# Layer 2 of a two-layer MLP after attention: visits over a rolling window of weight pairs, and additions shared out between VectorE and GpSimd by waiting time

## The chip, the cores and the metric

The kernel runs on one core of a Trainium2 chip. The metric is the device time of one execution in microseconds (us). Names: PE is TensorE (PEld its weight loads), ACT ScalarE, DVE VectorE, POOL GpSimd, SP the queue that issues the transfers.

## What is computed

Attention over 2304 tokens (4 batches of 576, 8 heads of 64) gives x [2304, 512]. Then two layers follow, in float32:

```
x = _moe_ref(x, w_in, w_out, alpha)     # h = x @ w_in; g = max(h,0) + alpha*min(h,0); g @ w_out
y = _moe2_ref(x, w_in, w_out)           # h = x @ w_in; g = h if h>0 else exp(h)-1;    g @ w_out
```

Both layers go from 512 to 2048 features and back to 512. The weights arrive as 64-bit floats.

## The kernel before

**Numbers in two halves.** A float32 product is made of three TensorE products: every operand x is split into a high part xh (a copy by ACT, rounded by its type) and a low part xl = x - xh (a subtraction on another engine). So each tile that PE reads costs one ACT copy and one subtraction of 128x512.

**Layer 1** takes tokens in groups of 288; each of its steps s is one block of 128 features. Its element-wise work on DVE is r (the leaky ReLU) and gl (the low part of g), two instructions a step.

**Layer 2** works on *pairs* of feature blocks (256 features) and on groups of 512 tokens; the last group has 256. There are 8 pairs (NP2 in the change) and 5 groups (`NB2`; the small one is `HALF`). The up-projection of one pair and one group is a *unit* u: seven products by Strassen's scheme in Winograd's form (`upf`, L1610 on), then the exponential and the split of g (`th_el2`, `th_el3`), and the down-projection (`down2`) with accumulation over the pairs of a turn in four PSUM banks. A unit of the small group is done plainly (`uph`, `th_elh`). On DVE a full unit begins with the sum m (m<-s,bank), then e and three c, three n and two gl. PE may go on to the unit's last three products only when m, e and c are there. Units are numbered from u0; four units (`NJ`) make a *turn*, and there are ten turns, so 40 units.

**Two passes.** `turns` is a list of (h, z): pass h uses pairs 0 to 3 (h=0) or 4 to 7 (h=1), z is the token group. In pass 0 every group's partial output is stored to DRAM (`osp`), in pass 1 it is read back and added (`th_os`, `th_fin2`). The last group of pass 0 is the first of pass 1, and its prepared input is kept (`xof`), so nine inputs are prepared.

**Weight pairs.** SBUF holds four pairs (`wslot`). A pair's preparation (`th_conv_in`, `th_conv_out`) is: four transfers of raw 64-bit weights, 512 KB each (`th_ldw2`); for each of the four an ACT op and two DVE ops that turn 64 bits into 32 (`decode`: cp, then cw); four sums S of 128x256 for Strassen's scheme; and six splits (four wi, two wo). In pass 0 the four slots stay in use until the fifth turn has passed over them, so pairs 4 to 7 are all loaded and prepared while that turn and the next run (units u16 to u22).

**Token groups.** `th_x2` loads a group's input, makes four differences xt and seven splits xq; eleven subtractions of 128x512.

**Who subtracts.** The sums S, the wi splits, the xt, the xq and the eight additions x of group 0's partial input are on POOL, the wo splits and all of the element-wise chain on DVE.

**What sets the order.** The program is put in order when it is built: threads (`spawn`, with a priority) are advanced by a table of engine times in `_Clock`, and each engine then executes its list strictly in that order, waiting on semaphores. Threads of layer 2's chain have priorities near -100; the weights and groups have 2 and more, and fill what is free. The lines of the profile are all L246 because one helper (`_Engine`) issues everything; operations are told apart by their tiles.

Of the kernel before, what the change touches and what calls it, by code (L numbers as in the profile page):

```python
# [36 lines left out]
XR = 11  # L37
WARM = True
# [19 lines left out]
class _Clock:  # L58
# [10 lines left out]
    def __init__(self):  # L69
        self.cols, self.gear = {}, []  # L70
        self.t = dict.fromkeys(("PE", "ACT", "DVE", "SP", "DMA", "POOL"), 0.0)
        self.t["SP"] = 560.0
        self.hw = 0.0
        self.seen = {}
# [84 lines left out]
    def op(self, eng, cost, share, outs, ins, wait=0.0):  # L159
        outs, ins = [self.span(a) for a in outs], [self.span(a) for a in ins]  # L160
        t = max(self.t[eng], self.deps(eng, outs, ins) + wait)
        if share is not None:
            cost += 42.0 if share > 0.9 and self.share < 0.9 else 0.0
            self.share = share
        end = t + cost if share is None else self.pe(t, cost, share)
        self.note(eng, outs, ins, end)
        self.t[eng] = self.cur["t"] = end
        self.cur["on"] = eng
# [32 lines left out]
class _Engine:  # L201
# [3 lines left out]
    def cost(self, op, kw, args):  # L205
        if op == "transpose":
            return int(args[1].shape[0]) / 1.2 + 3, int(args[1].shape[0]) * int(args[0].shape[0]) / 16384
        if op == "matmul":
            n, m = _free(kw["out"]), int(kw["out"].shape[0])
            share = int(kw["lhsT"].shape[0]) * m / 16384  # L210
            if kw["lhsT"].dtype == BF16:
                return n / 2.4, share
            if kw["lhsT"].dtype == F32R:
                return max(n * 0.4375 + 7, m / 1.2 + 3), share
            if int(kw["lhsT"].shape[0]) == D and int(kw["lhsT"].offset) >= D * int(kw["lhsT"].ap[0][0]):
                return 8.0, share
# [12 lines left out]
        if op == "reciprocal":
            return 68 + n * 6.25, None  # L230
        fast = sb and op in ("tensor_scalar", "tensor_copy")
        ptr = op == "scalar_tensor_tensor" and not isinstance(kw["scalar"], (int, float))
        return 68 + n * (0.52 if fast else 1.0417) + (60 if ptr else 0), None

    def __getattr__(self, op):
        fn = getattr(self.eng, op)

        def call(*args, **kw):
            if op == "dma_start":
                self.clock.dma(kw["out"], kw["in_"])  # L240
            else:
                outs = [kw[k] for k in ("out", "accum_out") if k in kw] + list(args[:1])
                ins = [a for k, a in kw.items() if k not in ("out", "accum_out") and hasattr(a, "ap")]
                wait = 0.6 * int(kw["lhsT"].shape[1]) if op == "matmul" else 0.0
                self.clock.op(self.name, *self.cost(op, kw, args), outs, ins + list(args[1:]), wait)
            return fn(*args, **kw)  # L246
# [4 lines left out]
def fused_kernel(ctx: ExitStack, tc: tile.TileContext, qk, vt, vl, ql, kl, vb, w_in1, w_out1, alpha,  # L251
# [72 lines left out]
    def load_w(key, slot=None):  # L324
        ly, nm, f = key
# [422 lines left out]
    order = [z for z in range(1, HALF - 1)] + [0, HALF, HALF - 1]  # L748
    turns = [(0, z) for z in order] + [(1, z) for z in [HALF - 1] + list(range(HALF - 1)) + [HALF]]
# [44 lines left out]
    def advance(th):  # L794
# [19 lines left out]
        if w:  # L814
            if w[0] == "bank":
                return False
            t = ck.t[w[0]]
# [416 lines left out]
    def part(t, x, eng):  # L1234
        n = _free(x)
        ACT.activation(out=t[:, 0, 0:n], in_=x, func=AF.Copy)
        yield (eng.name,)
        eng.tensor_tensor(out=t[:, 1, 0:n], in0=x, in1=t[:, 0, 0:n].bitcast(F32), op=ALU.subtract)

    def th_conv_in(h, j):  # L1240
        f = h * NF // 2 + 2 * j
        for z in range(2):
            yield from decode((2, "i", f + z))
        x, y = tmp.pop((2, "i", f)), tmp.pop((2, "i", f + 1))
# [3 lines left out]
        for o, p, q, op in ((0, a21, a22, ALU.add), (1, S[:, 0], a11, ALU.subtract), (2, a11, a21, ALU.subtract),  # L1248
                            (3, a12, S[:, 1], ALU.subtract)):
            yield ("POOL",)  # L1250
            POOL.tensor_tensor(out=S[:, o], in0=p, in1=q, op=op)
        st["W", h, j] = w = []
        for z, src in enumerate((x, S[:, 0:2].rearrange("p s c -> p (s c)"), S[:, 2:4].rearrange("p s c -> p (s c)"), y)):
            yield "key", "fr", h, wslot[j][z]
            yield ("ACT",)
            w.append(w_slot(wslot[j][z], f"wi{h}{j}{z}"))
            yield from part(w[z], src, POOL)
# [3 lines left out]
        finish("wi", h, j)  # L1261

    def th_conv_out(h, f):
        key = (2, "o", h * NF // 2 + f)
        yield from decode(key)
        yield ("ACT",)
        st["Wo", h, f] = w_slot(wslot[f // 2][4 + f % 2], f"wo{h}{f}")
        yield from part(st["Wo", h, f], tmp.pop(key), DVE)
        put("cw")
        finish("wo", h, f)  # L1270

    def th_ldw2():
        for h in range(2):
            for j in range(NJ):
                for nm, z in (("i", 0), ("i", 1), ("o", 0), ("o", 1)):
                    slot = wslot[j][z + (4 if nm == "o" else 0)]
                    yield "key", "fr", h, slot
                    yield ("DMA",)
                    key = (2, nm, h * NF // 2 + 2 * j + z)
                    load_w(key, slot)  # L1280
                    finish("ld", key)
                    ck.cur["t"] = now[0]
# [114 lines left out]
    def th_x2(i, z):  # L1397
# [20 lines left out]
        if not z:  # L1418
            for kt in range(KT):
# [3 lines left out]
                yield ("POOL",)  # L1423
                POOL.tensor_tensor(out=t[:, kt, :G1], in0=t[:, kt, :G1], in1=p[:, :G1], op=ALU.add)
# [3 lines left out]
        def diff(x, y, out=None):  # L1428
            o = cp["pool"].tile([128, 2, U2], F32, tag="xt", name="xt", bufs=2) if out is None else out
            POOL.tensor_tensor(out=o, in0=x, in1=y, op=ALU.subtract)  # L1430
            return o

        def split2(k, x):
# [15 lines left out]
            yield ("POOL",)  # L1449
            POOL.tensor_tensor(out=q[:, 1], in0=x, in1=q[:, 0].bitcast(F32), op=ALU.subtract)  # L1450
# [7 lines left out]
        yield ("POOL",)  # L1458
        t1 = diff(b12, b11)
        yield ("POOL",)  # L1460
        t2 = diff(b22, t1)
# [3 lines left out]
        yield ("POOL",)  # L1465
        t3 = diff(b22, b12)
# [3 lines left out]
        yield ("POOL",)  # L1470
        diff(b21, t2, t2)
# [90 lines left out]
    def uph(u, f):  # L1562
        i, j = divmod(u, NJ)
        h, z = turns[i]
        bk = bank[(5, 6)[u % 2] if f else (4, 7)[u % 2]][:, :U2]
        xi = xof[i]
        if not f:
# [3 lines left out]
            run_until("wi", h, j)  # L1571
# [3 lines left out]
        at(done["wi", h, j], done["x2", xi, 0], done["x2", xi, 1])  # L1575
        for k in range(2):
            q = st["x2", xi, k]
            for a in range(2):
                for b, (pw, px) in enumerate(P3):
                    PE.matmul(out=bk,  # L1580
                              lhsT=st["W", h, j][3 * f][:, HL[pw], (2 * k + a) * 128:(2 * k + a + 1) * 128],
# [9 lines left out]
    def up2(u, late):  # L1591
        i, j = divmod(u, NJ)
        h, z = turns[i]
# [4 lines left out]
        if late and i == NB2 - 1:  # L1598
            for z in range(4):
                ck.cur["t"] = ck.t["PE"]  # L1600
                finish("fr", 1, wslot[j][z])

    def upf(u, late):
        i, j = divmod(u, NJ)
        h, z = turns[i]
# [3 lines left out]
        if not late:  # L1609
# [3 lines left out]
            run_until("wi", h, j)  # L1613
        xi = xof[i]
        for k, (w, o) in enumerate(PROD):
# [6 lines left out]
            t = [done["wi", h, j], done["x2", xi, k]]  # L1622
# [4 lines left out]
            for a in range(2):  # L1627
                for b, (pw, px) in enumerate(P3):
                    PE.matmul(out=outs[k], lhsT=st["W", h, j][w][:, HL[pw], o + a * 128:o + (a + 1) * 128],
# [3 lines left out]
            if j == NJ - 1 and not (i + 1 < len(turns) and xof[i + 1] == xi):  # L1633
# [6 lines left out]
    def down2(u, f):  # L1640
        i, j = divmod(u, NJ)
        h, z = turns[i]
        run_until("gu", u, f)
        run_until("wo", h, 2 * j + f)
        gh, gl = gs["u", u]
        W2 = st["Wo", h, 2 * j + f]
        t = [done["gu", u, f], done["wo", h, 2 * j + f]]
        for m in range(size[z] // 128):
            if not j and not f:
                last = i - 1 if not i or m < size[turns[i - 1][1]] // 128 else i - 2  # L1650
# [10 lines left out]
        if i == NB2 - 1:  # L1661
            ck.cur["t"] = ck.t["PE"]
            finish("fr", 1, wslot[j][4 + f])

    def th_os(i):
        c0 = turns[i][1] * G2
        for m in range(size[turns[i][1]] // 128):
            yield "tok", "os"
            yield "key", "part", turns[i][1], m
# [6 lines left out]
    def th_fin2(i, m):  # L1676
        h, z = turns[i]
# [24 lines left out]
    xof = list(range(NB2)) + [NB2 - 1] + list(range(NB2, 2 * NB2 - 1))  # L1702

    with tc.manual_schedule():
# [68 lines left out]
        for s in range(NS1):  # L1773
# [5 lines left out]
            if s == T7:  # L1779
# [6 lines left out]
                for h in range(2):  # L1786
                    for j in range(NJ):
                        spawn(th_conv_in(h, j), 2 + h + j / 10)
                        for z in range(2):
                            spawn(th_conv_out(h, 2 * j + z), 2.05 + h + j / 10 + z / 100)  # L1790
                for k in range(2 * NB2 - 1):
                    spawn(th_x2(k, turns[k + (k >= NB2)][1]), 2.02 + k)
# [44 lines left out]
        for u in range(NU2):  # L1837
            slot[0] = NS1 + u
            i, j = divmod(u, NJ)
            if turns[i][0] and j == NJ - 2:  # L1840
# [102 lines left out]
```

## Time and profile before

| | us |
|---|---|
| median of three runs | 961.65 (959.56 to 962.97) |
| profiled execution | 963.32 |
| its span, first to last instruction | 961.5 |
| busy: PE, DVE, ACT, POOL | 920.6, 660.7, 502.5, 190.8 |
| first unit of layer 2 on PE, from | 554.4 |
| last matmul group, from | 957.5 |

Busy PE counts time in which a matmul is in flight. Where the table of stages shows PE below the length of the stage, PE stood still. DVE's busy time includes time in which an instruction was held up after its start. The granted clock (PEclk) is a share of 2.4 GHz.

### The profile page before, as it was taken

The numbers are of one execution on the slowest core, as the hardware profiler recorded it, in microseconds if no ns is written. First come the engines' busy times: TensorE is split into PE (matmuls) and PEld (weight loads), VectorE is DVE, ScalarE is ACT, GpSimd is POOL, SyncE is SP. The second block draws the span as 40 slices with busy tenths as digits, with TensorE's granted clock in tenths as the row PEclk, the third lists the DMA queues.
The fourth block names the chain that finished last, engine by engine and source line by source line (L and its number), as shares of the span: only waits on it lengthen the run. The fifth ranks groups of instructions, "written<-read, shape, count | busy, mean of one in ns | idle before, by whom it ended". The sixth has DMA issues, their size and how long they took to land. (4 is left out here: it accounts for less than half of the span.)

```text
span 961.5 us, 17703 instructions
## 1 busy us (share of the span) xinstructions
PE 920.6 (96%) x6841; PEld 845.0 (88%) x6841; DVE 660.7 (69%) x1336; ACT 502.5 (52%) x1291; POOL 190.8 (20%) x157
## 2 busy tenths in 40 slices
PE   7988999999999999999999989999999999999998
PEld 4677898899999999999999978998997788999987
DVE  5897874536959799899637886545458985454543
ACT  5786884554444562323236566445556565455343
POOL 0000000000000000000106775532444545342000
PEclk8789899999999999999999999999999999999999
DMA  9673735225231412101112631211225332140202
GB/s 272 203 282 119 263 146 72 101 58 167 70 77 49 141 54 92 44 7 61 46 32 85 216 113 43 71 47 64 100 79 176 110 110 89 44 132 22 89 1 87
DMA packets 65530, 96.94 MB, mean 101 GB/s; under 512 B 25794, under 2 KB 41538, under 8 KB 65266
## 3 DMA queue, kind: packets, MB, share of 16 engines
q1 hardware_dynamic: 65446, 95.81, 31.9%
q8 instruction: 53, 0.87, 0.4%
q14 instruction: 31, 0.25, 0.1%
HBM read 77.46 MB, written 19.78 MB: 101 GB/s over the span
## 5 line engine op out<-in xcount | busy, mean ns | idle before, releaser
L246 PE MATMUL bank<-xh,wi 128*128 128x288 f32 x1024 | 241.8, 304 | 5.8 <-DVE wi L246 3.6
L246 PE MATMUL bank<-gh,wo 128*128 128x288 f32 x1024 | 233.6, 301 | 0.1
L246 PEld LDWEIGHTS bank<-xq,wi 128*128 128x128 f32 x1536 | 196.4, 193 | 14.9 <-DVE m L246 4.7
L246 PE MATMUL bank<-xq,wi 128*128 128x256 f32 x1536 | 200.4, 285 | 6.5 <-DVE m L246 3.8
L246 PEld LDWEIGHTS bank<-xh,wi 128*128 128x128 f32 x1024 | 175.4, 190 | 13.3 <-DVE wi L246 5.0
L246 PE MATMUL bank<-wo,gh 128*128 128x512 f32 x576 | 180.6, 395 | 4.3 <-ACT gh L246 4.3
L246 ACT ACTIVATE n<-bank 128x288 f32<-128x288 f32 (+1 forms) x176 | 70.7, 402 | 215.6 <-PE bank L246 214.4
L246 PEld LDWEIGHTS bank<-gh,wo 128*128 128x128 f32 x1024 | 173.4, 189 | 3.4 <-issue 2.1
L246 PE MATMUL bank<-gl,wo 128*128 128x288 f32 x512 | 151.6, 296 | 2.0 <-DVE gl L246 2.0
L246 PE MATMUL bank<-xl,wi 128*128 128x288 f32 x512 | 152.3, 297 | 0.1
L246 PEld LDWEIGHTS bank<-wo,gh 128*128 128x128 f32 x576 | 103.9, 190 | 22.6 <-ACT gh L246 5.2
L246 POOL TENSOR_TENSOR xt<-x 128x512 f32<-128x512 f32 x14 | 18.6, 1330 | 487.7 <-ACT n L246 474.2
L246 PE MATMUL bank<-wo,gl 128*128 128x512 f32 x288 | 113.5, 394 | 1.0 <-DVE gl L246 1.0
L246 DVE SCALAR_TENSOR_TENSOR r<-n,nal,bank 128x288 f32<-128x288 f32 x128 | 65.3, 510 | 65.1 <-ACT n L246 64.9
L246 PEld LDWEIGHTS bank<-gl,wo 128*128 128x128 f32 x512 | 97.1, 190 | 2.5 <-DVE gl L246 2.5
L246 PEld LDWEIGHTS bank<-xl,wi 128*128 128x128 f32 x512 | 97.3, 190 | 0.6 <-DVE xl L246 0.6
L246 ACT ACTIVATE gh<-r 128x288 fp32r<-128x288 f32 x128 | 56.6, 442 | 65.7 <-DVE r L246 65.6
L246 DVE TENSOR_TENSOR c<-m,bank 128x256 f32<-128x256 f32 x64 | 26.4, 419 | 87.6 <-PE bank L246 87.6
L246 DVE TENSOR_TENSOR gl<-r,gh 128x288 fp32r<-128x288 f32 x128 | 64.5, 504 | 19.5 <-ACT gh L246 18.9
L246 DVE TENSOR_TENSOR gl<-n,gh 128x512 fp32r<-128x512 f32 (+1 forms) x80 | 60.1, 754 | 12.1 <-ACT gh L246 10.8
L246 PEld LDWEIGHTS bank<-wo,gl 128*128 128x128 f32 x288 | 54.5, 189 | 15.1 <-DVE gl L246 3.3
L246 ACT ACTIVATE gh<-n 128x512 fp32r<-128x512 f32 (+1 forms) x80 | 46.3, 582 | 14.5 <-DVE n L246 14.4
(116 smaller groups left out, 1268.4 us busy)
## 6 DMA issues: line engine op xcount, KB each, us to landing
rawi<-in_w_in_dram SPq DMA_DIRECT2D x32, 512.0 KB
rawo<-in_w_out_dram SPq DMA_DIRECT2D x32, 512.0 KB
qk<-in_qk_dram SPq DMA_DIRECT2D x12, 582.0 KB
osp<-os SPq DMA_DIRECT2D x18, 256.0 KB
os<-osp SPq DMA_DIRECT2D x18, 256.0 KB
out_dram<-os SPq DMA_DIRECT2D x18, 256.0 KB
yT<-ys SPq DMA_DIRECT2D x28, 144.0 KB
x<-yT SPq DMA_DIRECT2D x7, 576.0 KB
```

Source lines behind the costliest of these rows:

```text
L246: return fn(*args, **kw)
```

## The change

**Visits.** `turns` becomes a list of visits (z, w): group z is worked with the four pairs w to w+3, counted without end, where pair q holds the features of pair q mod 8. The window moves on by one pair from one visit to the next (by none from the fifth to the sixth). Each group is still visited twice and sees all eight pairs; pairs 8 to 11 are pairs 0 to 3 again, loaded and prepared a second time. `lastv[q]` is the last visit that uses pair q; after it the slot q mod 4 is given on. `again[i]` tells a second visit, which adds the stored partial output. Every visit prepares its own group input, so ten are prepared.

**Additions.** `pick` chooses, when the program is built, between DVE and POOL for every S, wi, wo, xt, xq and x: POOL only where by the table of engine times it would be done more than 1.2 us ahead of DVE (`BIAS`). The table also learns that DVE and POOL instructions of certain kinds do not run at the same time (`port`).

```diff
-    order = [z for z in range(1, HALF - 1)] + [0, HALF, HALF - 1]
-    turns = [(0, z) for z in order] + [(1, z) for z in [HALF - 1] + list(range(HALF - 1)) + [HALF]]
+    turns = [(1, 0), (2, 1), (0, 2), (3, 3), (1, 4), (HALF, 4), (2, 5), (0, 6), (3, 7), (HALF, 8)]
+    NQ = turns[-1][1] + NJ
+    lastv = [max(i for i, (z, w) in enumerate(turns) if w <= q < w + NJ) for q in range(NQ)]
+    again = [any(y == z for y, _ in turns[:i]) for i, (z, w) in enumerate(turns)]
...
+    def port(self, other, t, cost):
+        while True:
+            hit = [b for a, b in self.ports[other][-24:] if a < t + cost and t < b]
+            if not hit:
+                return t
+            t = max(hit)
...
+    def pick(n):
+        c = ck.cur["t"]
+        return POOL if max(c, ck.t["POOL"]) + 150 + 2.25 * n < max(c, ck.t["DVE"]) + 68 + 1.04 * n + BIAS else DVE
...
-        eng.tensor_tensor(out=t[:, 1, 0:n], in0=x, in1=t[:, 0, 0:n].bitcast(F32), op=ALU.subtract)
+        pick(n).tensor_tensor(out=t[:, 1, 0:n], in0=x, in1=t[:, 0, 0:n].bitcast(F32), op=ALU.subtract)
...
-            yield ("POOL",)
-            POOL.tensor_tensor(out=S[:, o], in0=p, in1=q, op=op)
+            yield ("ANY",)
+            pick(256).tensor_tensor(out=S[:, o], in0=p, in1=r, op=op)
...
-            POOL.tensor_tensor(out=o, in0=x, in1=y, op=ALU.subtract)
+            pick(2 * U2).tensor_tensor(out=o, in0=x, in1=y, op=ALU.subtract)
...
     def th_ldw2():
-        for h in range(2):
-            for j in range(NJ):
...
+        for q in range(NQ):
...
-        if late and i == NB2 - 1:
+        if late and lastv[q] == i:
...
-    xof = list(range(NB2)) + [NB2 - 1] + list(range(NB2, 2 * NB2 - 1))
...
+                for q in range(NQ):
+                    p = 2 + max(0, q - NJ + 1) + q / 100
+                    spawn(th_conv_in(q), p + .1)
+                    for z in range(2):
+                        spawn(th_conv_out(q, z), p + .2 + z / 1000)
+                for k, (z, _) in enumerate(turns):
+                    spawn(th_x2(k, z), 2.05 + k)
```

**Counts.** PE's instructions are the same in number. DVE has 197 more: 16 cp, 16 cw, 39 S, 41 wi, 6 wo, 47 xq, 26 xt, 6 x. POOL keeps 39 of its 153 additions, ACT has 47 more (16 cp, 24 wi and wo, 7 xq). SP issues 16 more transfers of raw weights (512 KB each) and three more for a group's input (1 MB).

**Where it moves instructions.** DVE at the end of layer 1, up to the first m of layer 2 (r and gl are layer 1's chain; cp, cw, wo and S belong to weight pairs). Before:

```order
L246 SCALAR_TENSOR_TENSOR r<-n,nal,bank_71 128x288
L246 TENSOR_SCALAR cp<-cp 128x512
L246 SCALAR_TENSOR_TENSOR cw<-rawi_7034,cp 128x512
L246 TENSOR_TENSOR gl<-r,gh 128x288
L246 TENSOR_TENSOR wo_7120<-cw,wo_7120 128x512
L246 TENSOR_SCALAR cp<-cp 128x512
L246 SCALAR_TENSOR_TENSOR cw<-rawi_7065,cp 128x512
L246 TENSOR_TENSOR m<-s_7154,bank_70 128x256
```

Changed:

```order
L262 SCALAR_TENSOR_TENSOR r<-n,nal,bank_71 128x288
L262 SCALAR_TENSOR_TENSOR cw<-rawo_7009,cp 128x512
L262 TENSOR_TENSOR S<-S,cw 128x256
L262 TENSOR_TENSOR wo_7088<-cw,wo_7088 128x512
L262 TENSOR_TENSOR gl<-r,gh 128x288
L262 TENSOR_TENSOR S<-cw 128x256
L262 TENSOR_SCALAR cp<-cp 128x512
L262 SCALAR_TENSOR_TENSOR cw<-rawi_7030,cp 128x512
L262 TENSOR_TENSOR m<-s_7142,bank_70 128x256
```

After the last gl there stood a split, a cp and a cw ahead of m; now a sum S of POOL's, a cp and a cw.

DVE in unit u2 of the changed kernel, up to the first m of u3 (wi and wo are the splits of weight pairs):

```order
L262 TENSOR_TENSOR wo_7455<-cw,wo_7455 128x512
L262 TENSOR_TENSOR wi_7461<-S,wi_7461 128x512
L262 TENSOR_TENSOR gl<-n,gh 128x512
L262 SCALAR_TENSOR_TENSOR n<-n,c 128x512
L262 TENSOR_SCALAR cp<-cp 128x512
L262 SCALAR_TENSOR_TENSOR cw<-rawi_7255,cp 128x512
L262 TENSOR_TENSOR wi_7479<-S,wi_7479 128x512
L262 TENSOR_TENSOR gl<-n,gh 128x512
L262 TENSOR_SCALAR cp<-cp 128x512
L262 SCALAR_TENSOR_TENSOR cw<-rawo_7302,cp 128x512
L262 TENSOR_TENSOR wi_7491<-cw,wi_7491 128x512
L262 TENSOR_TENSOR m<-s_7510,bank_73 128x256
```

Before, unit u2 held no weight work on DVE at all; now the three last of these wi are pair 3's, which u3 is the first to use.

DVE in the middle, unit u18. Before (from its third instruction):

```order
L246 TENSOR_TENSOR c<-e,bank_72 128x256
L246 TENSOR_TENSOR gl<-n,gh 128x512
L246 TENSOR_TENSOR wo_8910<-cw,wo_8910 128x512
L246 TENSOR_SCALAR cp<-cp 128x512
L246 SCALAR_TENSOR_TENSOR cw<-rawo_8861,cp 128x512
L246 TENSOR_SCALAR cp<-cp 128x512
L246 SCALAR_TENSOR_TENSOR cw<-rawi_8886,cp 128x512
L246 TENSOR_TENSOR c<-m,bank_71 128x256
L246 TENSOR_TENSOR wo_8951<-cw,wo_8951 128x512
L246 TENSOR_TENSOR c<-m,bank_72 128x256
L246 TENSOR_SCALAR cp<-cp 128x512
L246 SCALAR_TENSOR_TENSOR n<-n,bank_70 128x256
```

Changed (the whole unit):

```order
L262 TENSOR_TENSOR m<-s_9252,bank_70 128x256
L262 TENSOR_TENSOR e<-m,bank_71 128x256
L262 TENSOR_TENSOR c<-e,bank_72 128x256
L262 TENSOR_TENSOR c<-m,bank_71 128x256
L262 TENSOR_TENSOR c<-m,bank_72 128x256
L262 SCALAR_TENSOR_TENSOR n<-n,bank_70 128x256
L262 SCALAR_TENSOR_TENSOR n<-n,c 128x256
L262 SCALAR_TENSOR_TENSOR n<-n,c 128x512
L262 TENSOR_TENSOR gl<-n,gh 128x512 x2
L262 TENSOR_TENSOR xq_9337<-xt,xq_9337 128x512
```

The work on pairs 4 and 5 is gone from here, and one xq of POOL's has come.

## Rows read from the trace of the kernel before

**Rows 1.** The page, part 1: busy time, share and instructions of each engine.

```profile
PE 920.6 (96%) x6841; PEld 845.0 (88%) x6841; DVE 660.7 (69%) x1336; ACT 502.5 (52%) x1291; POOL 190.8 (20%) x157
```

**Rows 2.** Stages: length, then busy us of PE, PEld, DVE, ACT, POOL; PEclk; DMA share; GB/s.

```profile
520.00:600.00 80.00, 72.41 (x484) 67.41 (x483) 63.61 (x93) 48.68 (x100) 54.90 (x44) 0.98 0.35 109
600.00:735.00 135.00, 135.00 (x855) 122.37 (x854) 74.68 (x136) 70.61 (x144) 53.62 (x45) 1.00 0.26 83
735.00:800.00 65.00, 57.69 (x332) 48.88 (x331) 55.56 (x86) 39.03 (x77) 36.14 (x30) 0.97 0.34 113
800.00:940.00 140.00, 140.00 (x875) 126.67 (x874) 73.56 (x147) 65.17 (x126) 34.41 (x26) 1.00 0.21 70
```

**Rows 3.** Waits of PE, 480 to 600 us: total us, times, longest.

```profile
PE bank L246 <- DVE m L246: 3.3, 1, 3.3
...
PE bank L246 <- ACT gh L246: 0.7, 1, 0.7
```

**Rows 4.** Waits of PE, 735 to 800 us.

```profile
PE bank L246 <- ACT gh L246: 3.6, 3, 1.6
```

**Rows 5.** Busy time by stage, finer: the stretches with a lower granted clock.

```profile
560.00:570.00 10.00, 6.81 (x43) 6.82 (x44) 6.98 (x11) 4.62 (x11) 7.65 (x8) 0.83 0.38 113
...
760.00:780.00 20.00, 17.56 (x96) 14.78 (x95) 18.38 (x29) 11.56 (x24) 9.31 (x8) 0.91 0.49 159
```

**Rows 6.** Timeline of DVE: pair 0's first cw, the last split before m, and m.

```profile
505.83 0.69 DVE L246 SCALAR_TENSOR_TENSOR cw<-rawi,cp 128x512 uint32<-128x512 uint32 x1
...
557.94 1.78 DVE L246 TENSOR_TENSOR wo<-cw,wo 128x512 fp32r<-128x512 f32 x1
...
562.72 0.41 DVE L246 TENSOR_TENSOR m<-s,bank 128x256 f32<-128x256 f32 x1
```

**Rows 7.** Groups of DVE instructions by form, 735 to 800 us: busy us, mean ns.

```profile
L246 DVE TENSOR_SCALAR cp<-cp 128x512 uint32<-128x512 uint32 x13 | 11.1, 853 | 0.0
L246 DVE TENSOR_TENSOR gl<-n,gh 128x512 fp32r<-128x512 f32 x10 | 8.8, 893 | 1.2 <-ACT gh L246 1.2
L246 DVE SCALAR_TENSOR_TENSOR cw<-rawo,cp 128x512 uint32<-128x512 uint32 x7 | 8.6, 1230 | 0.2
L246 DVE TENSOR_TENSOR wo<-cw,wo 128x512 fp32r<-128x512 f32 x8 | 8.0, 1000 | 0.8 <-ACT wo L246 0.8
...
L246 DVE TENSOR_TENSOR c<-m,bank 128x256 f32<-128x256 f32 x10 | 3.8, 411 | 0.0
```

**Rows 8.** Timeline of POOL and DVE, one meeting: start us, length us.

```profile
757.63 1.30 POOL L246 TENSOR_TENSOR wi<-cw,wi 128x512 fp32r<-128x512 f32 x1 [4.81 <-ACT wi L246]
...
757.67 1.80 DVE L246 SCALAR_TENSOR_TENSOR n<-n,c 128x512 f32<-128x512 f32 x1
```

**Rows 9.** Timeline of DVE where nothing holds it up.

```profile
545.27 0.42 DVE L246 TENSOR_SCALAR cp<-cp 128x512 uint32<-128x512 uint32 x1
545.68 0.69 DVE L246 TENSOR_TENSOR wo<-cw,wo 128x512 fp32r<-128x512 f32 x1
546.29 0.45 DVE L246 TENSOR_TENSOR gl<-r,gh 128x288 fp32r<-128x288 f32 x1
...
579.59 0.42 DVE L246 SCALAR_TENSOR_TENSOR n<-n,bank 128x256 f32<-128x256 f32 x1 [0.21 <-ACT n L246]
579.93 0.42 DVE L246 SCALAR_TENSOR_TENSOR n<-n,c 128x256 f32<-128x256 f32 x1
```

**Rows 10.** Timeline of PE in undisturbed units: two full, then two half stages.

```profile
589.34 3.04 PE L246 MATMUL bank<-xq,wi 128*128 128x256 f32 x24
...
599.86 3.04 PE L246 MATMUL bank<-xq,wi 128*128 128x256 f32 x24
...
692.58 1.59 PE L246 MATMUL bank<-xq,wi 128*128 128x256 f32 x12
...
695.40 1.59 PE L246 MATMUL bank<-xq,wi 128*128 128x256 f32 x12
```

**Rows 11.** Timeline of DVE: the first sum of a full unit, u3.

```profile
592.97 0.42 DVE L246 TENSOR_TENSOR m<-s,bank 128x256 f32<-128x256 f32 x1
```

More of the change, by code (lines that the diff above doesn't have):

```diff
@@ L37 @@
 XR = 11
+BIAS = -1200.0
+NP2 = NF // 2
 WARM = True
@@ L73, in __init__ @@
         self.hw = 0.0
+        self.ports = {"DVE": [], "POOL": []}
         self.seen = {}
@@ L157, in note, with op @@
                 uses[r0, r1, lo, hi, src, write] = end
-    def op(self, eng, cost, share, outs, ins, wait=0.0):
+    def port(self, other, t, cost):
[4 more added lines that the diff above has]
+            t = max(hit)
+    def op(self, eng, cost, share, outs, ins, wait=0.0, port=False):
         outs, ins = [self.span(a) for a in outs], [self.span(a) for a in ins]
@@ L164, in op @@
             self.share = share
+        if port:
+            t = self.port("POOL" if eng == "DVE" else "DVE", t, cost)
+            self.ports[eng].append((t, t + cost))
         end = t + cost if share is None else self.pe(t, cost, share)
@@ L244, in call @@
                 wait = 0.6 * int(kw["lhsT"].shape[1]) if op == "matmul" else 0.0
-                self.clock.op(self.name, *self.cost(op, kw, args), outs, ins + list(args[1:]), wait)
+                sb = sum(kw[k].space != bass.MemoryType.PSUM for k in ("in0", "in1", "in_") if k in kw)
+                port = self.name == "POOL" or self.name == "DVE" and (
+                    sb > 1 or sb == 1 and op in ("tensor_scalar", "tensor_copy"))
+                self.clock.op(self.name, *self.cost(op, kw, args), outs, ins + list(args[1:]), wait, port)
             return fn(*args, **kw)
@@ L816, in advance @@
                 return False
-            t = ck.t[w[0]]
+            t = min(ck.t["DVE"], ck.t["POOL"]) if w[0] == "ANY" else ck.t[w[0]]
             if c["on"] != w[0] and c["t"] > (now[0] if w[0] == "DMA" else max(now[0], t)) + (DMG if slot[0] >= 0 else DMG0):
@@ L1260, in th_conv_in, with th_conv_out @@
         put("S")
-        finish("wi", h, j)
-    def th_conv_out(h, f):
-        key = (2, "o", h * NF // 2 + f)
+        finish("wi", q)
+    def th_conv_out(q, z):
+        key = (2, "o", q % NP2 * 2 + z, q)
         yield from decode(key)
         yield ("ACT",)
-        st["Wo", h, f] = w_slot(wslot[f // 2][4 + f % 2], f"wo{h}{f}")
-        yield from part(st["Wo", h, f], tmp.pop(key), DVE)
+        st["Wo", q, z] = w_slot(wslot[q % NJ][4 + z], f"wo{q}{z}")
+        yield from part(st["Wo", q, z], tmp.pop(key))
         put("cw")
-        finish("wo", h, f)
+        finish("wo", q, z)
     def th_ldw2():
-        for h in range(2):
-            for j in range(NJ):
[L1275 to L1282, printed above, removed]
+        for q in range(NQ):
+            for nm, z in (("i", 0), ("i", 1), ("o", 0), ("o", 1)):
+                slot = wslot[q % NJ][z + (4 if nm == "o" else 0)]
+                yield "key", "fr", q // NJ, slot
+                yield ("DMA",)
+                key = (2, nm, q % NP2 * 2 + z, q)
+                load_w(key, slot)
+                finish("ld", key)
+                ck.cur["t"] = now[0]
     def th_ldw():
@@ L1448, in split2 @@
             ACT.activation(out=q[:, 0], in_=x, func=AF.Copy)
[L1449 to L1450 removed]
+            yield ("ANY",)
+            pick(2 * U2).tensor_tensor(out=q[:, 1], in0=x, in1=q[:, 0].bitcast(F32), op=ALU.subtract)
             finish("x2", i, k)
@@ L1457, in th_x2 @@
             return
[L1458 to L1461, printed above, removed]
+        t1 = yield from diff(b12, b11)
+        t2 = yield from diff(b22, t1)
         yield from split2(0, t2)
@@ L1464, in th_x2 @@
         yield from split2(2, t1)
-        yield ("POOL",)
-        t3 = diff(b22, b12)
+        t3 = yield from diff(b22, b12)
         yield from split2(3, t3)
@@ L1469, in th_x2 @@
         yield from split2(5, b22)
-        yield ("POOL",)
-        diff(b21, t2, t2)
+        yield from diff(b21, t2, t2)
         put("x2")
@@ L1632, in upf @@
             finish("pp", u, k)
-            if j == NJ - 1 and not (i + 1 < len(turns) and xof[i + 1] == xi):
+            if j == NJ - 1:
                 put("xr")
@@ L1641, in down2 @@
         i, j = divmod(u, NJ)
-        h, z = turns[i]
+        z, wq = turns[i]
+        wq += j
         run_until("gu", u, f)
-        run_until("wo", h, 2 * j + f)
+        run_until("wo", wq, f)
         gh, gl = gs["u", u]
-        W2 = st["Wo", h, 2 * j + f]
-        t = [done["gu", u, f], done["wo", h, 2 * j + f]]
+        W2 = st["Wo", wq, f]
+        t = [done["gu", u, f], done["wo", wq, f]]
         for m in range(size[z] // 128):
             if not j and not f:
-                last = i - 1 if not i or m < size[turns[i - 1][1]] // 128 else i - 2
+                last = i - 1 if not i or m < size[turns[i - 1][0]] // 128 else i - 2
                 run_until("fin2", last, m)
@@ L1660, in down2 @@
             tick()
-        if i == NB2 - 1:
+        if lastv[wq] == i:
             ck.cur["t"] = ck.t["PE"]
-            finish("fr", 1, wslot[j][4 + f])
+            finish("fr", wq // NJ + 1, wslot[wq % NJ][4 + f])
     def th_os(i):
-        c0 = turns[i][1] * G2
-        for m in range(size[turns[i][1]] // 128):
+        c0 = turns[i][0] * G2
+        for m in range(size[turns[i][0]] // 128):
             yield "tok", "os"
-            yield "key", "part", turns[i][1], m
+            yield "key", "part", turns[i][0], m
             yield ("SP",)
```

68 lines of the change are left out of this document (32 added, 36 removed).

## Prediction

> **What bounds the kernel now.** I read the busy times first, then the table by stage, then what PE waits for in the stages where it stands, then the engine it waits for. PE is busy for 96% of the span [rows 1], so only its idle time and its clock can be won. By stage [rows 2], PE has no idle time from 600 to 735 and from 800 to 940 us. It loses 80.00 - 72.41 = 7.6 us from 520 to 600, at the change of layers, and 65.00 - 57.69 = 7.3 us from 735 to 800, where pairs 4 to 7 are prepared. What follows the last matmul group (from 957.5 of 961.5 us) is the output's way out, and stays. At the change of layers the longest wait is 3.3 us for one DVE sum, m [rows 3]; in the middle it is 3.6 us for three gh [rows 4], which ACT makes from what DVE delivers. Around both stands the granted clock falls [rows 5]: a mean of 0.83 over 10 us is 3.4 us at the lower level (1.2 instead of 2.4 GHz), which loses 1.7 us of work, and 0.91 over 20 us is 3.6 us, which loses 1.8. Together 7.6 + 7.3 + 3.5 = **18.4 us** are to be had.
>
> **Why DVE is late.** From 735 to 800 us DVE is busy for 55.56 of 65 us and POOL for 36.14 [rows 2]. The same DVE instructions take far longer there than where nothing holds them: a cp 853 ns instead of 420, a wo 1000 and a cw 1230 instead of 690 [rows 7, 9]. Sums with one operand in PSUM (c<-m,bank) stay at 411 [rows 7]. One meeting shows it whole: an n of 0.69 us starts 0.04 us after a POOL wi of 1.30 us and lasts 1.80 [rows 8]. So DVE stands still while POOL reads. Over four forms: 13 x 0.43 (cp) + 10 x 0.20 (gl) + 7 x 0.54 (cw) + 8 x 0.31 (wo) = 13.9 us lost for 30 POOL instructions, 0.46 us each. The 3.3 us wait has this cause too: wo, cp and cw, 1.8 us of work, take from 557.94 to 562.72, 4.8 us, before m [rows 6].
>
> **The cost on DVE of what is moved.** Back to back, an instruction of 512 elements takes 0.61 us from start to start (545.68 to 546.29), one of 256 takes 0.34, and a cp 0.41 to 0.45 [rows 9]. By these paces a unit's own chain is 5 x 0.34 + 2 x 0.34 + 3 x 0.61 = 4.2 us of the 10.52 that PE takes for a full unit [rows 10]. A pair costs DVE 4 x (0.45 + 0.61) + 4 x 0.34 + 6 x 0.61 = 9.3 us if all is done there, a token group 11 x 0.61 = 6.7. A visit of four units (42.1 us) with one pair, one group and 2.4 for the partial sums then needs 16.8 + 9.3 + 6.7 + 2.4 = 35.2 us, 84%, less what POOL keeps. The whole addition is 120 x 0.69 + 39 x 0.42 + 6 x 0.45 + 16 x 0.42 + 16 x 0.69 = 119 us; about 114 POOL instructions fewer give back 114 x 0.46 = 52 at most. So DVE should show 725 to 755 us busy, where it showed 661 [rows 1].
>
> **Removed: the middle.** The preparation of four pairs within six units is spread over the whole layer. In the order of the change, the units from u16 to u19 have 4.8 to 6.7 us on DVE. The stands of 7.3 and the clock's 1.8 go: **-9.1 us**.
>
> **Change of layers.** From pair 0's first cw to the first m, DVE's list holds 42.5 us by these paces, where it held 30.0, and POOL has next to nothing left there. Now that stretch lasts from 505.83 to 562.72 us [rows 6], 56.9, of which PE stands 3.3 before m [rows 3] and 3.6 in small pieces (7.6 less 3.3 and less 0.7 for a gh, [rows 3]); so PE needs 50, and DVE is 85% full but no longer held up. Of the 3.6 I keep 1.0, between 0 (the lists fit) and 3.6 (as now). For m's own wait of 3.3: behind the last gl are now an S, a cp and a cw, 1.4 us instead of 4.8, and one POOL split falls there (up to 1.3). I keep 0.6, between 0 and 1.3.
>
> **Added: unit u2.** Here the list has 13.6 us for DVE between the sums m of u2 and u3, against PE's 10.5. Pair 3's second wi, which u3's first product reads, stands 17 instructions behind u2's m, 8.4 us by the paces. An m starts 3.6 us after its unit (592.97 against 589.34) [rows 10, 11], so this wi is ready near 12.0 us; u3 should start at 10.5. That is a new stand of 1.5. The third wi follows 2.9 us behind, and the 18 matmuls ahead of its use take 2.3, which adds 0.6. Two POOL additions placed there bring 2 x 0.46. Together **3.0 us**, between 0.7 (the gh that is late here now) and 4.7 (if POOL's two block in full, 2 x 1.3). If the clock falls behind it, 1.0 of its 1.7.
>
> **Added: full units later.** Eight units (u4, u7, u10, u14, u26, u30, u33, u34) have 8.8 to 10.2 us on DVE. Bounds per unit: nothing, as from 600 to 735 us, where DVE was at 74.68 of 135 [rows 2]; and (7.3 + 1.8) / 6.2 units = 1.45 us, as from 735 to 800. They lie nearer the second in load, but meet about 1 POOL instruction each instead of 5, and their weight work is due a visit later, so I take 0.4: **3.2 us**. The small group's units hold at most 5.3 us for 2 x 2.82 [rows 10].
>
> Edits without cost: ACT's 47 more at 0.55 us are 26 us on an engine at 52% [rows 1]. The 16 transfers more and the extra group are 9.4 MB over 380 us, 25 GB/s beside the 70 to 113 there [rows 2]; each is due six units after its slot is free. On SP's queue a raw transfer that waits for its slot holds the stored partials and group inputs behind it; these have a unit and more of time.
>
> **The sum**: -18.4 + 1.0 + 0.6 + 3.0 + 1.0 + 3.2 = -9.6 us. The profiled execution (963.32, span 961.5) would be 953.7; it lay 1.7 above the median, and the median of 961.65 becomes **952.0**.
>
> The Trainium skill has a rule that speaks against this change (Perfetto Trace Analysis, Optimizing Scalar/DVE Operations): where DVE is saturated, giving some work to ScalarE or even GpSimd may make sense. By it alone the additions brought back would be pure load. The same section adds that the two share a read port, so that moving work between them might not help; rows 7 and 8 agree with that half, and by the rule alone the first rival below would hold.
>
> **The rivals.**
> 1. *DVE becomes the bound (slower).* The 18 units behind u3 with 7.4 us or more on DVE each lose 1.45 us, as the middle does now: -18.4 + 5.6 (change of layers) + 26.1 = +13.3, **975.0**. It decides from 12.8 / 18 = 0.7 us a unit. For it: DVE executes in order, and at 85% busy PE lost that much. Against: POOL's share of that was 13.9 of 55.6 us, and POOL keeps 39 of 153. Chance 0.12.
> 2. *The new waits eat the gain.* The same with 0.55 to 0.87 us a unit (12.8 less and more 2.9, by 18): 958.8 to 964.5, about **961.6**. Chance 0.10.
> 3. *Only the middle is won.* At the change of layers DVE has 42.5 us of work and stays as late as now: -9.1 + 2.3 (u2, less the 0.7) + 3.2 = -3.6, **958.1**. For it: the list there is 12.5 us longer. Against: rows 6. Chance 0.20, of which 0.08 ends within 0.3%.
> 4. *All fits.* The lists keep DVE ahead, only 2.0 us at u2 remain: -16.4, **945.3**. For it: units at half load lost nothing [rows 2]. Chance 0.13.
>
> **How the numbers follow.** My forecast has 0.45, itself from 948 to 957. A measurement tells 0.3% (2.9 us) from no change. Faster: 0.45 + 0.13 + 0.12 = 0.70; same: 0.10 + 0.08 = 0.18; slower: 0.12. The range reaches from case 4 to the upper part of case 2, 945 to 963; it leaves out case 1, the end of case 2 and what lies below case 4, 0.19 in all.
>
> **What would show it.** Right: PE idle below 1 us in every 65 us around u16 to u22; cp, gl and cw near 0.42 and 0.69 us; POOL near 50 us busy; the longest PE wait of layer 2 on a wi or its ACT copy at u3; PEclk at 1.00 in the middle. Wrong: waits of PE on gh, gl or m spread over all visits (rival 1), long waits before u0 as now (rival 3), or PE waiting for raw weights through DVE's cp.

## The result and the profile after

The changed kernel takes **947.3 us** (median of four runs, 944.47 to 950.86) beside 962.31 of the kernel before in the same measurement: a ratio of 0.985, 95% interval 0.9809 to 0.9891, a gain of 15.0 us. The prediction was 952.0, range 945 to 963, faster with 0.70. So the direction and the range held; the gain is larger than the 9.6 us of the sum and lies between the forecast and rival 4 (945.3). Below, the profiled execution of 944.47 us (span 942.7) is read against that of before (span 961.5).

The page's first part for the changed kernel, which answers to [rows 1]:

```profile
PE 911.1 (97%) x6841; PEld 839.7 (89%) x6841; DVE 729.7 (77%) x1533; ACT 526.3 (56%) x1338; POOL 51.2 (5%) x43
```

DVE and POOL came out as forecast (725 to 755, near 50). Four of POOL's instructions are there in every version, so 39 are additions.

Busy time by stage of the changed kernel, columns as in [rows 2]:

```profile
520.00:600.00 80.00, 75.55 (x515) 70.16 (x515) 73.89 (x143) 52.52 (x106) 11.18 (x8) 1.00 0.45 143
600.00:735.00 135.00, 134.93 (x844) 121.91 (x843) 116.09 (x221) 85.96 (x167) 19.80 (x16) 1.00 0.36 112
735.00:800.00 65.00, 64.70 (x408) 58.38 (x408) 44.91 (x93) 36.40 (x75) 3.87 (x3) 1.00 0.31 107
800.00:920.00 120.00, 119.46 (x746) 107.79 (x745) 97.30 (x188) 70.28 (x137) 13.50 (x10) 1.00 0.32 105
```

The middle, which lost 7.3 us, loses 0.3, at a granted clock of 1.00. From 600 to 735 us DVE is now busy for 116.09 of 135 us, 86%, more than in the middle before (55.56 of 65, 85%), and PE stands for 0.07 us: a DVE at 86% is no bound here. What is left lies mostly at the change of layers, 4.45 us.

PE's waits in the changed kernel, 480 to 600 us, beside [rows 3], and 735 to 800 us, beside [rows 4]:

```profile
PE bank L262 <- DVE wi L262: 1.7, 2, 1.0
PE bank L262 <- ACT gh L262: 1.6, 1, 1.6
PE bank L262 <- ACT wi L262: 0.9, 1, 0.9
PE bank L262 <- DVE m L262: 0.2, 1, 0.2
...
PE bank L262 <- DVE gl L262: 0.3, 1, 0.3
```

DVE's forms from 735 to 800 us, which answer to [rows 7]:

```profile
L262 DVE TENSOR_TENSOR gl<-n,gh 128x512 fp32r<-128x512 f32 x8 | 6.2, 774 | 0.9 <-ACT gh L262 0.7
...
L262 DVE TENSOR_SCALAR cp<-cp 128x512 uint32<-128x512 uint32 x5 | 2.1, 422 | 0.2 <-ACT cp L262 0.2
...
L262 DVE SCALAR_TENSOR_TENSOR cw<-rawo,cp 128x512 uint32<-128x512 uint32 x2 | 1.4, 688 | 0.0
```

A cp is back at 422 ns (853 before) and a cw at 688 (1230), the lengths of [rows 9]; of the forms of [rows 7] only the gl is still held up (774, where f2 below, with no addition on POOL, has 686), with three POOL instructions left in the stage.

**Where the time went.** Three marks split the two spans; a plus is time won.

| stretch | before | after | won |
|---|---|---|---|
| start to the last xl of layer 1 | 498.32 | 495.33 | +3.0 |
| to u0's last three products on PE | 64.87 | 56.68 | +8.2 |
| to u4 on PE | 36.67 | 39.74 | -3.1 |
| to the end | 361.64 | 350.95 | +10.7 |

The first 3.0 us are not the change's: the program is the same there, with the same order on PE and DVE; what differs is the granted clock of the first 200 us (0.92 before, 0.95 after). Among the profiled executions of all kernels here it lies between 0.89 and 0.96, and the last xl starts between 495.0 and 500.7 us, so spans of single executions can differ by up to 5.7 us ahead of layer 2. For the experiments I therefore also give the length of layer 2, from the last xl to the sum m of u35, the last full unit: 422.91 us before, 406.98 after, won 15.9. From that m to the end both take the same (40.3 and 40.4).

The stand before u0's last products is gone. Here they run as soon as u0's own down-projection of layer 1 is through (PE of the changed kernel; m had begun at 551.21):

```profile
551.88 0.29 PE L262 MATMUL bank<-gh,wo 128*128 128x288 f32 x1
552.01 5.20 PE L262 MATMUL bank<-xq,wi 128*128 128x256 f32 x42
```

The loss behind it is two stands. The first was not in the prediction. It is at u0's down-projection, which PE reaches after u1's first products; timeline of all engines:

```profile
552.73 0.69 DVE L262 TENSOR_TENSOR wi<-cw,wi 128x512 fp32r<-128x512 f32 x1
...
553.33 0.42 DVE L262 TENSOR_SCALAR cp<-cp 128x512 uint32<-128x512 uint32 x1
...
553.84 0.69 DVE L262 SCALAR_TENSOR_TENSOR cw<-rawi,cp 128x512 uint32<-128x512 uint32 x1
...
555.11 0.69 DVE L262 TENSOR_TENSOR wi<-S,wi 128x512 fp32r<-128x512 f32 x1
555.71 0.68 DVE L262 TENSOR_TENSOR xt<-x 128x512 f32<-128x512 f32 x1
...
556.48 1.28 POOL L262 TENSOR_TENSOR xt<-x,xt 128x512 f32<-128x512 f32 x1 [5.74 <-DVE xt L262]
556.65 2.00 DVE L262 SCALAR_TENSOR_TENSOR n<-n,c 128x256 f32<-128x256 f32 x2
558.08 0.63 ACT L262 ACTIVATE gh<-n 128x512 fp32r<-128x512 f32 x1 [0.64 <-DVE n L262]
...
558.76 0.73 PE L262 MATMUL bank<-wo,gh 128*128 128x512 f32 x2 [1.55 <-ACT gh L262]
```

Between u0's first c and its n, DVE's list holds five instructions of weights and group, 3.2 us, and then a POOL xt lies across two n (2.00 us for what takes 0.34 + 0.42). So gh comes late, and PE waits 1.55 us for it. The second is the stand at u3 that the prediction had at 3.0 us, on the tiles it named:

```profile
578.39 0.50 PE L262 MATMUL bank<-xq,wi 128*128 128x256 f32 x2 [0.92 <-ACT wi L262]
579.68 2.41 PE L262 MATMUL bank<-xq,wi 128*128 128x256 f32 x18 [0.79 <-DVE wi L262]
583.04 0.74 PE L262 MATMUL bank<-xq,wi 128*128 128x256 f32 x4 [0.95 <-DVE wi L262]
...
586.74 1.46 PE L262 MATMUL bank<-xq,wi 128*128 128x256 f32 x10 [0.23 <-DVE m L262]
```

0.92 + 0.79 + 0.95 + 0.23 = 2.9 us.

**What a stand costs.** The view's idle time is not all that a stand costs. PE of the kernel before, at one stand:

```profile
551.75 0.42 PE L246 MATMUL bank<-gh,wo 128*128 128x288 f32 x2
552.86 0.40 PE L246 MATMUL bank<-gl,wo 128*128 128x288 f32 x1 [0.68 <-DVE gl L246]
553.09 0.43 PE L246 MATMUL bank<-gh,wo 128*128 128x288 f32 x2
...
553.49 0.43 PE L246 MATMUL bank<-gh,wo 128*128 128x288 f32 x2
```

By the start times the first three of these matmuls take 1.34 us (551.75 to 553.09) and the next three of the same kind 0.40 (553.09 to 553.49). So 0.94 us are lost where the view puts 0.68 of idle time: 0.26 more. At 15 of the 17 stands of layer 2 in that execution the start times give 0.26 to 0.28 more than the idle time; the other two run into the lower clock. The view lists 17 stands in layer 2 of the kernel before and 7 in the changed one.

### The profile page after: what moved, and what is told of

Read it like the earlier page. It is cut to its first block, busy times and chain, and to the rows that moved or that the text cites. A ratio compares the mean times of both kernels' runs of the same rounds, so it can differ in the third digit from the quotient of the medians.

```text
span 942.7 us, 17834 instructions
## 1 busy us (share of the span) xinstructions
PE 911.1 (97%) x6841; PEld 839.7 (89%) x6841; DVE 729.7 (77%) x1533; ACT 526.3 (56%) x1338; POOL 51.2 (5%) x43
## 5 line engine op out<-in xcount | busy, mean ns | idle before, releaser
L262 PE MATMUL bank<-xq,wi 128*128 128x256 f32 x1536 | 197.6, 283 | 3.0 <-DVE wi L262 1.7
L262 DVE TENSOR_TENSOR gl<-r,gh 128x288 fp32r<-128x288 f32 x128 | 58.7, 459 | 18.1 <-ACT gh L262 17.5
L262 DVE TENSOR_TENSOR gl<-n,gh 128x512 fp32r<-128x512 f32 (+1 forms) x80 | 56.8, 715 | 7.0 <-ACT gh L262 6.3
L262 ACT ACTIVATE gh<-n 128x512 fp32r<-128x512 f32 (+1 forms) x80 | 45.9, 581 | 15.9 <-DVE n L262 15.8
L262 ACT ACTIVATE n<-n 128x512 f32<-128x512 f32 (+1 forms) x80 | 47.2, 590 | 2.5
```

## The experiments

In short, theory 1: the gain is DVE's, which POOL holds up less; the visits matter because they take the four pairs out of the middle. Theory 2: the gain is the visits' alone, and who adds is of little account. Each kernel was timed beside the kernel before on the same chip. "Adds" is the number of POOL's instructions on the page, less four.

| kernel | adds | us | before | ratio, interval | layer 2, us | DVE busy |
|---|---|---|---|---|---|---|
| the change | 39 | 947.3 | 962.31 | 0.985 [0.9809, 0.9891] | 406.98 | 729.7 |
| the change again (f0) | 39 | 945.65 | 961.72 | 0.984 [0.9818, 0.9861] | 406.88 | 729.9 |
| visits only (e1) | 196 | 973.54 | 964.51 | 1.0083 [1.0051, 1.0114] | 433.24 | 710.2 |
| additions only (e2) | 17 | 950.05 | 964.51 | 0.9847 [0.982, 0.9873] | 412.89 | 691.2 |
| the same again (f1) | 17 | 951.17 | 961.72 | 0.9891 [0.9865, 0.9917] | 412.47 | 692.7 |
| visits, all on DVE (e3) | 0 | 943.69 | 964.51 | 0.978 [0.9747, 0.9813] | 403.98 | 728.8 |
| change, S in halves (e4) | 36 | 945.07 | 964.51 | 0.9793 [0.9759, 0.9827] | 405.12 | 727.5 |
| both of these (f2) | 0 | 941.84 | 961.72 | 0.9798 [0.9778, 0.9817] | 403.17 | 727.5 |
| two passes, all on DVE (f3) | 0 | 949.16 | 961.72 | 0.9883 [0.9854, 0.9913] | 411.28 | 692.8 |
| change, BIAS 0 (g1) | 125 | 955.23 | 964.28 | 0.9908 [0.9884, 0.9933] | 415.93 | 724.3 |
| change, no port rule (g2) | 28 | 946.57 | 964.28 | 0.9809 [0.9781, 0.9837] | 406.77 | 729.8 |

**Visits only (e1).** The change with the additions on their old engines and the table of engine times as before:

```diff
-            pick(256).tensor_tensor(out=S[:, o], in0=p, in1=r, op=op)
+            POOL.tensor_tensor(out=S[:, o], in0=p, in1=r, op=op)
...
-            yield from part(st["Wo", q, z], tmp.pop(key))
+            yield from part(st["Wo", q, z], tmp.pop(key), DVE)
```

> The visits with the rolling pairs, but every addition on the engine it had before (S, wi, xt, xq, x on GpSimd, wo on VectorE) and the table of engine times as before. Theory 1 (VectorE is late because it stands still while GpSimd reads; taking the additions off GpSimd is what wins): a visit of 42 us then has 21 GpSimd additions, which hold VectorE 21 x 0.46 = 9.7 us; the change of layers keeps its stands (7 us), and the visits spread stands over all turns: 957 to 968 us, cp and wo still at 0.8 to 1.2 us. Theory 2 (the burst of four pairs was the cause, spreading wins by itself): the middle's 9 to 11 us go, the change of layers stays: 952 us.

Slower than the kernel before, by 0.8%, and slower than either forecast. The page's first part, the stages and PE's waits from 800 us on:

```profile
PE 921.1 (95%) x6841; PEld 842.4 (87%) x6841; DVE 710.2 (73%) x1376; ACT 526.2 (54%) x1338; POOL 244.9 (25%) x200
```

```profile
520.00:600.00 80.00, 70.11 (x454) 64.06 (x455) 69.59 (x95) 47.92 (x97) 53.27 (x44) 0.96 0.41 126
600.00:735.00 135.00, 129.98 (x797) 114.74 (x796) 99.54 (x158) 79.70 (x156) 83.95 (x67) 1.00 0.31 99
735.00:800.00 65.00, 65.00 (x403) 58.57 (x403) 36.02 (x67) 34.46 (x72) 21.11 (x16) 1.00 0.39 129
800.00:940.00 140.00, 134.22 (x833) 119.41 (x832) 105.62 (x172) 81.63 (x161) 71.62 (x58) 1.00 0.30 99
```

```profile
PE bank L262 <- DVE m L262: 3.2, 3, 1.3
PE bank L262 <- ACT gh L262: 2.1, 2, 1.1
```

The stands of the old middle are gone (65.00 of 65), so the visits do what they say. But twelve smaller stands from 600 to 735 and from 800 to 940 us, most of them on m and gh, lose 5.0 + 5.8 = 10.8 us, more than the middle did. This is what rival 1 would look like, with POOL's additions as its cause: DVE does 157 additions fewer than in the change and is busy for only 19.5 us less. Theory 2 falls.

**Additions only (e2, and again as f1).** The kernel before with `pick`, `BIAS` and `port`, and nothing of the visits.

> The two passes as before, but the additions picked between VectorE and GpSimd as in the change, with its table of engine times. Theory 1: the change of layers wins its 5 us, and in the middle VectorE has 4 x 9.3 us for pairs and 6 x 4.2 for its chain in some 63 us, full but not held up: the stands there halve, 953 us. Theory 2: the middle stays as it was, since the burst stays: 957 us or more, PE idle 7 us from u16 to u22.

> Two passes with the picked additions, a second time, beside the change on one chip. If the visits are worth what the first profiles show (one stand of 4.4 us and 1.5 us of clock in the middle gone, 2 us lost at u3): 3 to 6 us above the change, ratio to before 0.988 to 0.991. If the visits are worth nothing once VectorE is not held up: the same time as the change.

Faster than either forecast. Most of the gain comes without the visits: 14.5 and 10.6 us. What the visits add was measured on one chip (f1 against f0): 951.17 - 945.65 = 5.5 us, intervals of the ratio apart. In layer 2 it is 5.6.

**All on DVE (e3).**

```diff
-BIAS = -1200.0
+BIAS = -1e9
```

> The change with every addition on VectorE, none on GpSimd. If the 39 additions left on GpSimd cost VectorE as much standing still (0.46 us each) as they take off it (0.61 each), the time stays: 945 to 949 us, the wait of 1.55 us at u1 is gone, the stand at u3 is 1 us longer. If GpSimd is needed where VectorE is full, the units with 9 us and more lose 0.5 to 1 us each: 953 us or more.

```profile
PE 913.7 (97%) x6841; PEld 842.4 (89%) x6841; DVE 728.8 (77%) x1572; ACT 526.1 (56%) x1338; POOL 0.2 (0%) x4
```

39 more additions on DVE, and DVE is busy for 728.8 us instead of 729.7. What POOL kept gave DVE no time back. The expectation missed at three points: the time is below its 945 to 949, the stand at u3 is shorter and not longer (0.54 us), and the wait that was to go is still there. The stand at u0's down-projection has another shape: PE waits 0.57 us for the gh and 0.85 for the gl behind it, 1.42 together, because DVE now makes both xt itself ahead of that gl. A gl in u4 has a new one of 0.93 us. PE in e3, at u0's down-projection:

```profile
561.73 0.73 PE L262 MATMUL bank<-wo,gh 128*128 128x512 f32 x2 [0.57 <-ACT gh L262]
563.31 0.50 PE L262 MATMUL bank<-wo,gl 128*128 128x512 f32 x1 [0.85 <-DVE gl L262]
```

So the meeting with POOL is not needed for that stand. By the first half of the rule that the prediction set against the change (the Trainium skill, Perfetto Trace Analysis, Optimizing Scalar/DVE Operations) POOL's share could have helped; DVE's 728.8 us beside 729.7 agree with its second half, that moving work between two engines with a shared read port might not help. The port itself is not seen in these numbers.

**S in two halves (e4), and with all on DVE (f2).** A pair's preparation begins its four sums in one tile S, which comes free when the pair's last wi is split, so the next pair's sums wait for that. Two tiles come free one after the other:

```diff
-        S = cp["pool"].tile([128, 4, 256], F32, tag="S", name="S", bufs=1)
+        Sa = cp["pool"].tile([128, 2, 256], F32, tag="Sa", name="Sa", bufs=1)
...
+            if o == 2:
+                yield "tok", "Sb"
+                Sb = cp["pool"].tile([128, 2, 256], F32, tag="Sb", name="Sb", bufs=1)
...
+            if z in (1, 2):
+                put(("Sa", "Sb")[z - 1])
```

> The change with the tile of a pair's four sums S cut into two tiles of two sums, each free for the next pair as soon as its own split is done. If the stand of 2.9 us before u3 comes from pair 3's sums waiting for pair 2's tile, pair 3 is ready in time and the stand goes: 944.5 us. If VectorE is simply full there (13.6 us of work in u2), the work only changes its order and 2 to 3 us of stand remain: 947 us.

> The changed kernel once more, as the measure for the three that follow on the same chip: 0.985 of the kernel before.

> The change with both mends: no addition on GpSimd, and the sums S in two tiles. If their wins add (3 us and 3 us of PE's stands): 6 us below the change, ratio 0.977 or less, PE standing below 2 us in all of layer 2. If one has taken the other's place: as the better of the two, ratio 0.978 to 0.980.

In e4 the stand at u3 is gone, except for 0.19 us on a gl, and the one at u0's down-projection stays with 1.58. f2 has the lowest time of this study, 3.8 us below the change on the same chip (by their ratios to the kernel before, it and e3 can't be told apart). Its second forecast came true: the two wins do not add, and PE still stands for 2.6 us in layer 2. Its stages and PE's waits from 480 to 800 us:

```profile
520.00:600.00 80.00, 78.46 (x540) 73.86 (x539) 75.05 (x157) 54.23 (x110) 0.00 (x0) 1.00 0.48 153
600.00:735.00 135.00, 133.92 (x841) 121.11 (x840) 114.29 (x234) 83.91 (x166) 0.00 (x0) 1.00 0.33 107
```

```profile
PE bank L262 <- DVE gl L262: 2.0, 3, 1.1
PE bank L262 <- ACT gh L262: 0.6, 1, 0.6
```

On the average of each form its wi, wo, gl and cw of 512 elements take 684 to 690 ns; none is held up. Beside e3 it wins 0.8 us in layer 2, which single executions can't tell from nothing; that S in halves helps by itself is shown by the stand at u3 that went, hardly by the time.

**Two passes, all on DVE (f3).**

> Two passes with every addition on VectorE, none on GpSimd. In the middle VectorE then has 4 x 9.3 us for pairs in one piece with its chain. If only being held up matters: 2 to 3 us below the two passes with picked additions. If the burst matters, the stand before u21 grows by the work that GpSimd did there (8 additions, 4 to 5 us): 2 to 5 us above them.

In time it is 2.0 us below f1, as the first forecast had it, though the intervals of the two ratios overlap; the stand in the middle grew all the same, from 3.79 to 5.55 us. PE's timeline in the middle, and its waits from 735 to 800 us:

```profile
764.27 5.41 PE L261 MATMUL bank<-xq,wi 128*128 128x256 f32 x24 [5.55 <-ACT wi L261]
```

```profile
PE bank L261 <- ACT wi L261: 5.9, 2, 5.6
PE bank L261 <- DVE wi L261: 0.4, 1, 0.4
```

With two passes 6.3 of PE's 7.8 us of idle time in layer 2 lie in the middle, where pairs 4 to 7 come at once, and the longest stand is longer than any of before. It also costs its clock: the 24 matmuls behind it take 5.41 us instead of 3.04 [rows 10], and the granted clock from 760 to 770 us is 0.66. So the visits are worth 949.16 - 941.84 = 7.3 us once POOL is out (S in halves included), and 411.28 - 403.98 = 7.3 in layer 2 against e3.

**How many additions POOL takes (g1 with BIAS 0, g2 without the port rule).**

```diff
-BIAS = -1200.0
+BIAS = 0.0
```

```diff
-        if port:
+        if False:
             t = self.port("POOL" if eng == "DVE" else "DVE", t, cost)
```

> The change with BIAS 0: POOL takes whatever it would end sooner by the table of engine times, 113 additions instead of 39; the visits stay. Theory A (every POOL addition that meets DVE work holds DVE up, so the price follows the count): between the 943.7 us with none and the 973.5 us with 180 in the same visits, that is 0.166 us each, 113 give about 962, no faster than the kernel before; DVE would show some 50 fewer additions' worth of work but no less busy time, near 725. Theory B (only those count that fall in the units just before or at the first use of a pair, as u1 to u3): most of the additional ones lie in later units with slack, the time is 946 to 950, and PE's idle time in layer 2 stays below 8 us.

> The change without the port rule in the table of engine times (the table then lets DVE and POOL run at the same time; 25 additions go to POOL). Theory A (the count decides): about as the change or better by (39 - 25) x 0.08 = 1 us, 944 to 946. Theory B (what the port rule does is to keep the meetings away from the tight units): slower than the change by 3 us or more, with stands of PE on gh, gl or m in u1 to u6.

The numbers of additions in these expectations are too low; the page has 125 for g1, 28 for g2 and 196 for e1. The page of g1, its clock behind the stand at u3, and PE's waits from 480 to 600 us:

```profile
PE 919.2 (96%) x6841; PEld 845.0 (88%) x6841; DVE 724.3 (76%) x1447; ACT 524.9 (55%) x1338; POOL 157.4 (16%) x129
```

```profile
580.00:590.00 10.00, 7.26 (x39) 6.22 (x37) 9.49 (x14) 8.91 (x17) 4.83 (x4) 0.87 0.00 0
```

```profile
PE bank L262 <- ACT wi L262: 1.9, 1, 1.9
PE bank L262 <- ACT gh L262: 1.6, 1, 1.6
...
PE bank L262 <- POOL wi L262: 0.8, 1, 0.8
```

Neither forecast for g1 came true: 955.23 is faster than before and slower than the change. In layer 2, against e3 (403.98), the additions cost 2.8 us for 28 (g2), 3.0 for 39 (the change), 11.9 for 125 (g1) and 29.3 for 196 (e1, whose table of engine times also differs): 0.08 to 0.10 us each in the first three, and 0.15 in e1. So the time goes with the count rather than with a few tight units, and theory A was right in kind and too dear for g1; whether e1's higher price comes from the count or from its table is not shown. With the engines the order of DVE's list changes too, in all of these runs; none moves additions with the order held. g2 is as fast as the change: the port rule in the table is not what wins the time, at this BIAS.

## Why the prediction was right, and where its sizes were off

**The mechanism held.** DVE was late because POOL held it up; taking the additions back cost DVE little, and spreading the pairs emptied the middle. Neither half does it alone: the visits by themselves are slower than before (e1), the additions by themselves keep a stand of 3.79 us in the middle (f1). The loss per POOL addition of 0.46 us, worked out from four forms of one stage, can be checked on the whole program: from e1 to e3 DVE gets 196 additions, about 120 us by the lengths of [rows 9] (48 S at 0.42, 140 at 0.69, 8 at 0.42), and is busy for only 728.8 - 710.2 = 18.6 us more; (120 - 18.6) / 196 = 0.52 us each.

**The sum, term by term** (gain as minus, by the marks of the table above):

| stretch | predicted | measured | what it was |
|---|---|---|---|
| change of layers, to u0's last products | -5.3 | -8.2 | the 1.0 and 0.6 kept were nothing |
| to u4 | +1.6 | +3.1 | 1.55 at u0 not seen; the clock's 1.0 did not come; four stands more at 0.26 |
| the rest | -5.9 | -10.7 | later units 0.84 for 3.2; eight stands fewer at 0.26 |
| together | -9.6 | -15.8 | |

The sum priced every stand at its idle time, and had no term for the 0.26 us on top of it. Ten stands fewer are 2.6 us. With 9.5 us of idle time (14.8 before, 5.3 after) and the clock's 3.5 they make 15.6 of the 15.9 us won in layer 2.

1. *Change of layers.* From 480 us to u0's last products PE has no wait at all. I kept 1.6 because DVE's list was 85% full there; the lower ends of both terms, nothing, were right. They are 1.6 of the 2.9 us by which the stretch did better; the other 1.3 fit what six stands cost beyond their 6.9 us of idle time.
2. *Unit u2/u3.* 3.0 forecast, 2.9 measured: 2.66 on pair 3's wi, at the place named, and 0.23 on the m behind them. The total agrees better than its parts. The forecast had 2.1 from the length of DVE's list and 0.92 from POOL; without POOL 0.54 are left (e3), with S in halves and POOL still there 0.19 (e4), and in g2 PE waits for no wi there. So the size hangs on the order and on tile S, which had no term, and that it was met is partly luck. The clock's 1.0 did not come: 1.00 throughout.
3. *Unit u0.* The accounting of the change of layers ended at the first m; u0's own chain behind it, from m to gl, had no term. In the change five instructions and one meeting lie in it, and PE waits 1.55 us there. The stand is in every run looked at but the kernel before: 1.42 without POOL (e3), 0.61 + 0.75 = 1.36 (f2), 0.18 + 0.76 = 0.94 with the two passes and no POOL (f3), 0.17 + 1.85 = 2.02 with the two passes and 17 additions on POOL (e2), and 1.30 + 1.42 = 2.72 in e1, where the additions are on their old engines. So neither the visits nor who adds makes it alone. In the kernel before, the weight work lay ahead of m, which was 3.26 us late; in the change m is in time and the work lies behind it, in u0's own chain. That this is the cause is argued from the lists: an order that keeps u0 free was not tried.
4. *Full units later.* The term that was mis-sized most: 3.2 us for eight units with 8.8 to 10.2 us on DVE, at 0.4 each; measured are 0.30 and 0.54, in u24 and u26, of which only u26 is among the eight. The lower bound, nothing, was the better one. The upper bound came from a stage where POOL blocked DVE, and e1, with 196 additions there, lost 10.8 us from 600 to 940: the price goes with POOL and not with DVE's load.
5. *The middle.* 10.7 + 0.84 = 11.5 won there and in the later units, where 9.1 was put down. 7.3 + 1.8 are idle time and clock as read; the other 2.4 stand in no wait. Eight stands fewer at 0.26 us are 2.1 of them. Another 0.34 lie in the 24 matmuls that took 3.38 us at 752.59 in the kernel before, beside 3.04 [rows 10]: one stand too short for the view to list, where the start times of the 12th to the 14th lie 0.37 and 0.22 us apart in place of 0.12.

Of the rivals, 1 is excluded for the change (PE stands for 0.07 us while DVE is 86% busy) and e1 shows what it looks like; 2 is excluded by the time and by the 0.84 us of the later units; 3 by the first stretch. Rival 4's "only 2.0 us at u2 remain" was nearest: 5.28 us of PE's idle time are left in layer 2.

## What to carry to other kernels

Where VectorE is late, first compare the length of its instructions with the same ones where the other engine is quiet; if they are stretched beside GpSimd, VectorE's load will hardly rise when it takes that work back, and the time may fall. When work bunched at one place is spread, the price of the loaded places afterwards is to be taken from places with the same load and the same neighbours, not from the bunch. What remains stands where a chain starts anew; there the in-order engine's list is to be priced unit by unit, from the first sum to the last tile that TensorE reads. And a stand of TensorE is worth more than the idle time that a profile shows for it: count the stands as well as their length.

## What the hardware did that was not expected

- VectorE at 86% busy over 135 us, executing strictly in order, cost TensorE 0.07 us; with all additions on it (f2) it was busy for 114.29 us there, and 1.08 us were lost.
- 39 two-input additions more on VectorE changed its busy time by -0.9 us (729.7 to 728.8).
- Each stand of TensorE cost 0.26 us more, by the start times, than the idle time that the profile shows for it.
- Behind one stand of 5.55 us the next 24 matmuls took 5.41 us in place of 3.04, 2.4 us more (f3); in g1 stands of 1.89, 0.85 and 0.86 us, one behind another, went with a granted clock of 0.87 over 10 us, while the three stands of 0.79 to 0.95 us of the change, on the same products, left it at 1.00.
- The granted clock of the first 200 us, the same program in all kernels, was between 0.89 and 0.96 from one execution to another, and the last xl of layer 1 started up to 5.7 us apart.
